# Moving the decay factors of a chunked linear attention to GpSimd, its result copies to ScalarE, and cutting its key-value product into 64x64 matmuls

## The chip, the cores and the metric

The kernel runs as one program on one core of one Trainium2 chip. The metric is the device time of one execution in microseconds (us). Three runs of the kernel before gave 903.01, 904.5 and 905.43 us; the median is 904.5 us.

The core has a matmul engine (TensorE, PE in the profile; its weight loads are shown as PEld), three engines for elementwise work (VectorE or DVE, ScalarE or ACT, GpSimd or POOL), and SyncE (SP), whose queue issues the DMAs here. Matmuls write PSUM banks; DVE and ACT read those banks; every operand of GpSimd in this kernel lies in SBUF.

## The reference

Three layers follow each other. The change touches the first one alone.

```python
# attention: q, k, v are (4 batches, 8 heads, 576 positions, 64)
scores = scale * np.matmul(q, k.transpose(0, 1, 3, 2))
gamma = 1.0 - 2.0 ** (-5.0 - np.arange(H, dtype=np.float32))
Dmat = np.where(rel >= 0, gamma[:, None, None] ** rel[None, :, :], 0.0)   # rel = i - j
attn = np.matmul(scores * Dmat[None], v)
# x = attn as 2304 tokens x 512
h = x @ w_in;  x = (h * np.cos(h)) @ w_out              # 512 -> 2048 -> 512
xn = x / rms(x) * rms_g
out = (silu(xn @ w_gate) * (xn @ w_val)) @ w_out2       # 512 -> 1536 -> 512
```

There is no softmax, so the decay gamma^(i-j) splits into gamma^i on the query side and gamma^(-j) on the values, and earlier positions can be summed up once as a state, the sum over j of key times value.

## The kernel before, in words

**Attention in 20 chunks.** Each batch is cut into five chunks of the sequence: four of 128 positions and a last one of 64 (`chunks`, `width`). `load(n)` brings a chunk in one DMA (the 64-wide one in two): keys `kt` and queries `qt` with the head dimension on the partitions, two heads per block of 128, values `vv` and keys once more `kk` with positions on the partitions. For each chunk:

- `scores(n)`: GpSimd multiplies the values by gamma^(-j) (L251); 8 matmuls make keys times queries, one per head, in 64-row halves of the array (L256), into two PSUM tiles; DVE copies each out through the causal mask (L259).
- `values(n)`: 4 matmuls of 128x128 add keys times values of each pair of heads to the tile `total` (L272), of which only the two 64x64 blocks on the diagonal are used; 4 matmuls apply the state of the earlier chunks to the queries (L277); ACT copies the two diagonal blocks of `total` into `state` (L282); 8 matmuls, one per head, add the masked scores times values (L287); DVE multiplies the result by `gam[c]`, which is gamma^i with the scale, on its way from PSUM to `xall` (L290). `gam[1]` to `gam[4]` are made once from `gam[0]` by ACT (L244).

All of this is in float32, so each of these matmuls shows twice in the trace: 8 matmuls are "x16".

**What runs beside it.** The first MLP goes in steps (token tile t, slice f of 128 hidden units). A step is 12 matmuls for the hidden slice (`hidden`, lines L193 to L195), the gate h*cos(h) on ACT and DVE (`gate_cos`: L431, L432, L434, L438, L440 and the difference on L130, which gives a high and a low part), and, three steps later, 12 matmuls of `out_t`. Weights arrive as 64-bit words of which float32 high and low parts are made (`Block.convert`: ACT L138, L147, L165; DVE L142, L143, L148, L149, L130), one block per hidden slice, 16 in all.

**Order of the work.** The first five chunks are the opening (`PRO`), with next to nothing beside them. Chunks 5 to 19 go two per step into steps 0 to 7 (`ATT_STEPS`), while the blocks are converted some steps ahead. After that the attention's PSUM and SBUF are given back, the last weight blocks are loaded, and the rest of the program (four more token tiles, the normalisation, the second MLP) follows. In this first part a scheduler puts each engine's instructions in one fixed order when the program is built; on the chip each engine works through its own list in that order and waits at an instruction until what it needs is there. Score tiles, attention results and hidden slices take turns in the three PSUM banks named `g` (`ps_tile`), so PE can begin a new one when an earlier one has been read out. SP's queue, in program order, loads chunk n+4 ahead of chunk n.

The lines that the change touches are L251 (behind it comes the new GpSimd instruction), L270 to L273 and L290.

Of the kernel before, what the change touches and what calls it, by code (L numbers as in the profile page):

```python
# [27 lines left out]
ALU = mybir.AluOpType  # L28
PSUM = bass.MemoryType.PSUM

P = 128
B, H, S, D = 4, 8, 576, 64
# [48 lines left out]
def body(ctx: ExitStack, tc, qkv, qkr, vr, w1, w2, rg, gq, gk, mask, out):  # L81
    nc = tc.nc
# [25 lines left out]
    def hidden_tile():  # L108
        return late["psh"].tile([P, 512], F32, tag="h", bufs=2, name="h")
# [4 lines left out]
    def ps_tile():  # L114
        if "psh" not in late:
            return psa.tile([P, 512], F32, tag="g", bufs=3, name="g")
        taken[0] += 1
        return hidden_tile() if taken[0] % 2 else acc_tile(KC + taken[0] // 2 % 2)
# [8 lines left out]
    xall = const.tile([P, KC, NT], F32, name="xall")  # L127
# [84 lines left out]
    ld, sc, total = {}, {}, {}  # L212
    gam0 = ap1.tile([P, NPAIR, P], F32, name="gam0")
    gam = [gam0]
# [31 lines left out]
    def scores(n):  # L246
        b, c = chunks[n]
        w = width(c)
        kt, qt, vv, _ = ld[n]
        v3 = vv[:w].rearrange("p (h d) -> p h d", h=H)  # L250
        nc.gpsimd.tensor_tensor(v3, v3, vg_sb[:w, c, :].unsqueeze(2).to_broadcast([w, H, D]), op=ALU.mult)  # L251
        ps = [ps_tile().rearrange("p (h i) -> p h i", h=NPAIR) for _ in range(2)]
        for p in range(NPAIR):
            for hh in range(2):
                r = slice(hh * D, (hh + 1) * D)
                nc.tensor.matmul(ps[hh][:w, p, :w], kt[r, p, :], qt[r, p, :], start=True, stop=True)  # L256
        for hh in range(2):
            s = ap.tile([P, NPAIR, P], F32, tag=f"s{hh}", bufs=2, name=f"s{hh}")
            nc.vector.tensor_tensor(s[:w, :, :w], ps[hh][:w, :, :w],  # L259
                                    mask_sb[:w, :w].unsqueeze(1).to_broadcast([w, NPAIR, w]), op=ALU.mult)  # L260
            sc[n, hh] = s

    def values(n):
        b, c = chunks[n]
        w = width(c)
        _, qt, vv, kk = ld.pop(n)
        if c < NFULL:
            if c == 0:
                total[0] = psa.tile([P, NPAIR, P], F32, tag="st", name="total")
            for p in range(NPAIR):  # L270
                cs = slice(p * P, (p + 1) * P)
                nc.tensor.matmul(total[0][:, p, :], kk[:, cs], vv[:, cs], start=c == 0 and p == 0, stop=True,  # L272
                                 skip_group_check=True)  # L273
        po = ps_tile().rearrange("p (a i) -> p a i", a=NPAIR)
        if c > 0:
            for p in range(NPAIR):
                nc.tensor.matmul(po[:, p, :w], state[:, p, :], qt[:, p, :], start=p == 0, stop=False,  # L277
                                 skip_group_check=True)
        if c < NFULL:
            for hh in range(2):  # L280
                r = slice(hh * D, (hh + 1) * D)
                nc.scalar.copy(state[r, :, r], total[0][r, :, r])  # L282
        for p in range(NPAIR):
            for hh in range(2):
                h = 2 * p + hh
                r = slice(hh * D, (hh + 1) * D)
                nc.tensor.matmul(po[r, p, :w], vv[:w, h * D:(h + 1) * D], sc[n, hh][:w, p, :w],  # L287
                                 start=c == 0 and p == 0, stop=True, skip_group_check=True)
        t0 = b * S + c * P
        nc.vector.tensor_tensor(xall[:, :, t0:t0 + w], po[:, :, :w], gam[c], op=ALU.mult)  # L290
        del sc[n, 0], sc[n, 1]

    warm = xsp.tile([P, 512], F32R, tag="xs", name="warm")
# [758 lines left out]
```

## Time and profile before

| | us |
|---|---|
| median of three runs | 904.5 (903.01 to 905.43) |
| the profiled execution, its own time | 904.74 |
| its span, first to last instruction | 902.9 |
| PE busy | 883.7 (98% of the span) |
| DVE busy | 669.0 (74%) |
| ACT busy | 478.3 (53%) |
| POOL busy | 96.3 (11%) |

The profiled execution is one run; 1.8 us of its time lie around the span. The attention takes the first 131 us of the span. Busy shares over the whole span say little about that stretch, so it is read by itself: the busy time of each engine between two points in time, then the instructions of one engine grouped by line and shape, then the order in time at single places. "A <- B" in a row of waits or in square brackets means that A stood idle until B had finished.

### The profile page before, as it was taken

What the parts mean: (1) busy time and instruction counts of PE and PEld (TensorE: products, weight loads), DVE (VectorE), ACT (ScalarE), POOL (GpSimd) and SP (SyncE); (2) the same over time, 40 slices, a digit from 0 to 9 for tenths busy, and PEclk for the clock granted to TensorE, in tenths of its full rate; (3) what the DMA queues carried; (4) which work ended last, traced back from release to release, by engine and by line L of the source; (5) the groups of instructions that cost most, each with busy time, mean ns of one, the idle gap of its engine ahead of it and who ended that gap; (6) DMA issues with size and microseconds to landing.
All of it is one profiled execution on the core that took longest, in us unless ns stands there. A gap on an engine that the chain in (4) does not pass through costs nothing.

```text
span 902.9 us, 14216 instructions
## 1 busy us (share of the span) xinstructions
PE 883.7 (98%) x5482; PEld 804.6 (89%) x5482; DVE 669.0 (74%) x999; ACT 478.3 (53%) x819; POOL 96.3 (11%) x99
## 2 busy tenths in 40 slices
PE   7999999999999999999999999999999999999998
PEld 6788778888887888998887899999999999999998
DVE  3999989678788887667777789789565589443584
ACT  4666566566565665456656665545443444333341
POOL 2331100000000000000434444200000000000000
PEclk9999999999999999999999999999999999999999
DMA  8966452044434444101568888998876788777793
GB/s 319 397 238 238 153 218 86 1 132 148 140 106 140 140 143 137 57 16 50 182 222 264 329 316 300 332 319 286 275 257 247 221 283 287 259 251 247 218 302 114
DMA packets 59027, 188.98 MB, mean 209 GB/s; under 512 B 5328, under 2 KB 23376, under 8 KB 50384
## 3 DMA queue, kind: packets, MB, share of 16 engines
q1 hardware_dynamic: 58960, 188.08, 61.2%
q8 instruction: 43, 0.70, 0.3%
q14 instruction: 24, 0.20, 0.1%
HBM read 140.87 MB, written 47.19 MB: 208 GB/s over the span
## 4 chain that ended last, share of the span: by engine, by line
PE 78%; DVE 14%; ACT 3%; issue 2%; DMA 1%; POOL 1%; SPq 0%; ACTq 0%; DVEq 0%; POOLq 0%
PE h L806 13%; PE acc L806 13%; PE acc L851 13%; PE acc L193 8%; PE acc L194 8%; PE acc L195 8%; PE h L193 3%; PE h L194 3%; PE h L195 3%; DVE w L130 3%; PE h L851 2%; DVE t L148 2%; DMA x<-qkv_dram 1%; DVE t L149 1%; PE g L287 1%
## 5 line engine op out<-in xcount | busy, mean ns | idle before, releaser
L806 PE MATMUL h<-w 128*128 128x384 f32 x720 | 139.9, 335 | 4.0 <-ACT s L772 2.7
L806 PE MATMUL acc<-w 128*128 128x384 f32 x720 | 140.1, 335 | 0.4
L806 PEld LDWEIGHTS h<-w 128*128 128x128 f32 x720 | 125.7, 188 | 5.9 <-ACT s L772 3.4
L806 PEld LDWEIGHTS acc<-w 128*128 128x128 f32 x720 | 125.5, 188 | 2.3 <-DVE v L794 2.3
L193 PE MATMUL acc<-ghi,w 128*128 128x512 f32 (+1 forms) x320 | 118.7, 371 | 1.5 <-ACT xall L662 1.4
L194 PE MATMUL acc<-glo,w 128*128 128x512 f32 (+1 forms) x320 | 118.2, 369 | 0.1
L195 PE MATMUL acc<-ghi,w 128*128 128x512 f32 (+1 forms) x320 | 117.8, 368 | 0.0
L851 PE MATMUL acc<-w 128*128 128x256 f32 x846 | 104.2, 283 | 0.0
L851 PEld LDWEIGHTS acc<-w 128*128 128x128 f32 x846 | 103.1, 191 | 0.3 <-DVE w L130 0.2
L434 ACT ACTIVATE r<-r,half_pi 128x512 f32<-128x512 f32 (+1 forms) x80 | 54.5, 681 | 61.7 <-DVE r L432 61.6
L529 POOL TENSOR_TENSOR z<-z 128x256 f32<-128x256 f32 x72 | 65.7, 914 | 156.7 <-DMA z<-w 94.4
L130 DVE TENSOR_TENSOR glo<-r,ghi 128x512 fp32r<-128x512 f32 (+1 forms) x78 | 52.2, 670 | 38.5 <-ACT ghi L440 38.0
L440 ACT CAST ghi<-r 128x512 fp32r<-128x512 f32 (+1 forms) x80 | 46.2, 577 | 54.8 <-DVE r L438 49.8
L193 PEld LDWEIGHTS acc<-ghi,w 128*128 128x128 f32 x320 | 60.3, 188 | 12.5 <-ACT xall L662 2.0
L195 PEld LDWEIGHTS acc<-ghi,w 128*128 128x128 f32 x320 | 60.3, 189 | 10.1
L194 PEld LDWEIGHTS acc<-glo,w 128*128 128x128 f32 x320 | 60.3, 188 | 10.0 <-DVE glo L130 0.3
L794 DVE TENSOR_TENSOR v<-s,acc 128x384 f32<-128x384 f32 x54 | 29.8, 552 | 52.7 <-PE acc L806 39.5
L834 ACT CAST w<-SV 128x768 fp32r<-128x768 f32 x55 | 42.4, 831 | 34.2 <-DVE SV L839 18.3
L130 DVE TENSOR_TENSOR w<-SV,w 128x768 fp32r<-128x768 f32 x55 | 50.1, 953 | 13.5 <-ACT w L834 13.5
L772 ACT COPY s<-h 128x384 f32<-128x384 f32 x54 | 25.8, 479 | 54.4 <-PE h L806 53.0
L193 PE MATMUL h<-xhi,w 128*128 128x512 f32 (+1 forms) x144 | 52.7, 366 | 0.0
L193 PE MATMUL acc<-xhi,w 128*128 128x512 f32 (+1 forms) x144 | 52.7, 366 | 0.0
(122 smaller groups left out, 1639.7 us busy)
## 6 DMA issues: line engine op xcount, KB each, us to landing
w<-so SPq DMA_DIRECT2D x42, 768.0 KB, 5.9
w<-s SPq DMA_DIRECT2D x24, 1024.0 KB, 4.9
raw<-w_dram SPq DMA_DIRECT2D x36, 512.0 KB, 4.1
w<-s SPq DMA_DIRECT2D x24, 768.0 KB, 4.3
raw<-w_dram SPq DMA_DIRECT2D x16, 1024.0 KB, 6.8
x<-qkv_dram SPq DMA_DIRECT2D x15, 1024.0 KB, 11.4
s<-w SPq DMA_DIRECT2D x12, 1024.0 KB, 6.2
w<-t SPq DMA_DIRECT2D x36, 256.0 KB, 2.4
```

The source lines that it names most:

```text
L130: eng.tensor_tensor(dst, src, hi.bitcast(F32), op=ALU.subtract)
L193: nc.tensor.matmul(dst, a[0], b[0], start=start, stop=False)
L194: nc.tensor.matmul(dst, a[0], b[1], start=False, stop=False)
L195: nc.tensor.matmul(dst, a[1], b[0], start=False, stop=stop)
L434: nc.scalar.activation(r, r, AF.Sin, bias=half_pi, scale=1.0)
L440: nc.scalar.copy(hi, r)
L529: nc.gpsimd.tensor_tensor(z[:, dst], z[:, a], z[:, b], op=op)
L772: nc.scalar.copy(t[:, :HALF], bank)
L794: nc.vector.tensor_tensor(t, s, bank, op=ALU.add)
L806: nc.tensor.matmul(bank, w[:, wp, kc * P:(kc + 1) * P], x[:, kc], start=k in (0, 1, 3) and kc == 0 and m == 0, stop=kc == 1 and m == 2, sk ...
L834: nc.scalar.copy(t[:, 0], src)
L851: nc.tensor.matmul(bank, s[:, a, i % 2, m * P:(m + 1) * P], wi[:, b], start=start and i == 0 and p == 0 and m % 2 == 0, stop=i == NPR - 1 ...
```

## The change

Four things change in `scores` and `values`:

1. Behind the scaling of the values, GpSimd multiplies the queries of the chunk in place by `gam[c]`, for all chunks but chunk 0. The score matmuls and the state matmuls then read scaled queries.
2. The result of every chunk but chunk 0 is copied from PSUM to `xall` by ACT, with no factor, in place of DVE's multiplication.
3. The product of keys and values is made per head: 8 matmuls of 64 columns by 64 columns in place of 4 of 128 by 128, the two heads of a pair in the two column halves of the array.
4. Chunk 0 keeps DVE's multiplication.

```diff
         nc.gpsimd.tensor_tensor(v3, v3, vg_sb[:w, c, :].unsqueeze(2).to_broadcast([w, H, D]), op=ALU.mult)
+        if n:
+            nc.gpsimd.tensor_tensor(qt, qt, gam[c], op=ALU.mult)
...
             for p in range(NPAIR):
-                cs = slice(p * P, (p + 1) * P)
-                nc.tensor.matmul(total[0][:, p, :], kk[:, cs], vv[:, cs], start=c == 0 and p == 0, stop=True,
-                                 skip_group_check=True)
+                for hh in range(2):
+                    h, r = 2 * p + hh, slice(hh * D, (hh + 1) * D)
+                    cs = slice(h * D, (h + 1) * D)
+                    nc.tensor.matmul(total[0][r, p, r], kk[:, cs], vv[:, cs], start=c == 0 and p == 0, stop=True,
+                                     skip_group_check=True)
...
-        nc.vector.tensor_tensor(xall[:, :, t0:t0 + w], po[:, :, :w], gam[c], op=ALU.mult)
+        if n:
+            nc.scalar.copy(xall[:, :, t0:t0 + w], po[:, :, :w])
+        else:
+            nc.vector.tensor_tensor(xall[:, :, t0:t0 + w], po[:, :, :w], gam[c], op=ALU.mult)
```

The scheduler lays the lists out anew. GpSimd's list for the first batch, as a difference (L251 scales values, the new L253 scales queries):

```order
-L251 TENSOR_TENSOR x<-x,gk_sb 128x512 x4
+L251 TENSOR_TENSOR x<-x,gk_sb 128x512 x2
+L253 TENSOR_TENSOR x<-x,gam_123 128x512
+L251 TENSOR_TENSOR x<-x,gk_sb 128x512
+L253 TENSOR_TENSOR x<-x,gam_145 128x512
+L251 TENSOR_TENSOR x<-x,gk_sb 128x512
+L253 TENSOR_TENSOR x<-x,gam_152 128x512
+L253 TENSOR_TENSOR x<-x,gam_162 128x256
 L251 TENSOR_TENSOR x<-x,gk_sb 64x512
```

Each scaling of queries stands directly behind (for the 64-wide chunk, ahead of) that of the chunk's values, and so ahead of the values of the next chunk.

DVE's list before, around the masks of chunk 6 (s_469 and s_471, L259) and the first gate (r, glo), with what each waits for:

```order
L290 TENSOR_TENSOR xall<-g,gam_162 128x4x64 [waits PE_49]
L142 TENSOR_SCALAR t<-t 128x1024
L259 TENSOR_TENSOR s_469<-g,mask_sb 128x512 [waits PE_49]
L143 TENSOR_SCALAR t<-t 128x1024 [waits DVE_49]
L148 SCALAR_TENSOR_TENSOR t<-raw,t 128x1024 [waits DMAHW6_49,DVE_49]
L432 SCALAR_TENSOR_TENSOR r<-r,g 128x512 [waits Activation_49]
L149 ISA t<-raw,t 128x2048 [waits DVE_49]
L259 TENSOR_TENSOR s_471<-g,mask_sb 128x512 [waits PE_49]
L438 TENSOR_TENSOR r<-g,r 128x512 [waits Activation_49]
L290 TENSOR_TENSOR xall<-g,gam_92 128x4x128 [waits PE_49]
L130 TENSOR_TENSOR w<-t,w 128x2x512 [waits Activation_49]
L130 TENSOR_TENSOR glo<-r,ghi 128x512 [waits Activation_49]
```

The same place in the changed kernel (the masks of chunk 6 are s_491 and s_493, L261; L439 and L445 are the old L432 and L438):

```order
L142 TENSOR_SCALAR t<-t 128x1024
L143 TENSOR_SCALAR t<-t 128x1024 [waits DVE_49]
L148 SCALAR_TENSOR_TENSOR t<-raw,t 128x1024 [waits DMAHW6_49,DVE_49]
L439 SCALAR_TENSOR_TENSOR r<-r,g 128x512 [waits Activation_49]
L149 ISA t<-raw,t 128x2048 [waits DVE_49]
L261 TENSOR_TENSOR s_491<-g,mask_sb 128x512 [waits PE_49]
L261 TENSOR_TENSOR s_493<-g,mask_sb 128x512 [waits PE_49]
L130 TENSOR_TENSOR w<-t,w 128x2x512 [waits Activation_49]
L445 TENSOR_TENSOR r<-g,r 128x512
L261 TENSOR_TENSOR s_531<-g,mask_sb 128x512 [waits PE_49]
L261 TENSOR_TENSOR s_533<-g,mask_sb 128x512 [waits PE_49]
L130 TENSOR_TENSOR glo<-r,ghi 128x512 [waits Activation_49]
```

The two results `xall` are gone from the list; the conversion of a block (L142, L143, L148, L149, then w) stands where it stood, and more of what is left lies between two steps of a conversion or a gate.

PE's list in the opening, changed kernel, from the products of chunk 0 on:

```order
L276 MATMUL total<-x 64x64 [waits DMAHW6_49,DMAHW4_49,Pool_49]
L276 MATMUL total<-x 64x64 x7
L258 MATMUL g<-x 128x128 [waits DMAHW7_49,Pool_49]
L258 MATMUL g<-x 128x128 [waits DVE_49]
L258 MATMUL g<-x 128x128 x6
L291 MATMUL g<-s_139,x 64x128 [waits DVE_49]
```

The scores of chunk 1 (L258, before L256) now wait for GpSimd as well as for their DMA, and chunk 0's own results (L291) stand behind them.

## Rows read from the trace of the kernel before

**Rows 1.** Busy us by stretch: PE, PEld, DVE, ACT, POOL; then clock, DMA, GB/s.

```profile
31.60:120.60 89.00, 84.58 (x734) 70.41 (x735) 87.64 (x115) 53.66 (x75) 19.52 (x13) 0.98 0.62 226
120.60:131.10 10.50, 10.50 (x79) 8.81 (x79) 7.89 (x12) 7.21 (x9) 0.00 (x0) 1.00 0.63 240
131.10:167.80 36.70, 36.70 (x163) 30.41 (x162) 33.19 (x43) 24.70 (x33) 0.00 (x0) 1.00 0.25 100
```

**Rows 2.** Timeline near the attention's end: start, us, engine, line, operation.

```profile
119.60 0.68 DVE L290 TENSOR_TENSOR xall<-g,gam 128x512 f32<-128x512 f32 x1
120.20 0.74 DVE L259 TENSOR_TENSOR s<-g,mask_sb 64x256 f32<-64x256 f32 x2
120.33 1.16 PE L277 MATMUL g<-x,state 128*128 128x128 f32 x8 [1.34 <-DVE xall L290]
122.45 0.50 PE L193 MATMUL g<-xhi,w 128*128 128x512 f32 x1
```

**Rows 3.** DVE from 24 to 131 us by line and shape: busy us, mean ns.

```profile
L149 DVE CUSTOM_DVE_ANT_0 t<-raw,t 128x2048 uint16<-128x2048 uint16 x12 | 15.4, 1283 | 0.0
L130 DVE TENSOR_TENSOR w<-t,w 128x1024 fp32r<-128x1024 f32 x10 | 14.6, 1462 | 0.0
L143 DVE TENSOR_SCALAR t<-t 128x1024 int32<-128x1024 int32 x11 | 8.4, 759 | 0.1
L130 DVE TENSOR_TENSOR glo<-r,ghi 128x512 fp32r<-128x512 f32 x7 | 5.6, 799 | 0.0
L130 DVE TENSOR_TENSOR xlo<-xall,xhi 128x512 fp32r<-128x512 f32 x4 | 3.8, 955 | 0.7 <-ACT xhi L187 0.7
```

**Rows 4.** Timeline, 31 to 35 us: DVE's differences beside one GpSimd scaling.

```profile
31.54 0.68 DVE L130 TENSOR_TENSOR xlo<-xall,xhi 128x512 fp32r<-128x512 f32 x1
32.14 1.21 DVE L130 TENSOR_TENSOR w<-t,w 128x1024 fp32r<-128x1024 f32 x1
32.27 1.98 POOL L251 TENSOR_TENSOR x<-x,gk_sb 128x512 f32<-128x512 f32 x1 [1.81 <-DMA x<-qkv_dram]
33.27 1.52 DVE L130 TENSOR_TENSOR xlo<-xall,xhi 128x512 fp32r<-128x512 f32 x1
```

**Rows 5.** Timeline, opening: chunk 1 and the factors.

```profile
9.53 4.57 ACT L244 ACTIVATE gam<-gam,gk_sb 128x128 f32<-128x128 f32 x16
...
11.38 1.69 PE L256 MATMUL g<-x 64*128 64x128 f32 x16 [1.28 <-DMA x<-qkv_dram]
11.40 1.04 POOL L251 TENSOR_TENSOR x<-x,gk_sb 128x512 f32<-128x512 f32 x1 [3.20 <-DMA x<-qkv_dram]
```

**Rows 6.** GpSimd from 24 to 131 us by line and shape.

```profile
L251 POOL TENSOR_TENSOR x<-x,gk_sb 128x512 f32<-128x512 f32 x12 | 17.2, 1432 | 52.1 <-DMA x<-qkv_dram 48.7 <-PE g L195 2.0 <-ACT state L282 1.4
L251 POOL TENSOR_TENSOR x<-x,gk_sb 64x512 f32<-64x512 f32 x3 | 4.9, 1617 | 11.8 <-DMA x<-vr_dram 11.8
```

**Rows 7.** GpSimd's products with two full operands, whole span: ns min/median/max, first and last start.

```profile
L130 POOL TENSOR_TENSOR glo<-r,ghi x2: 1304/1496/1688, 265.4 to 352.3; 128x512 fp32r<-128x512 f32 x2
L529 POOL TENSOR_TENSOR z<-z x72: 727/742/1528, 430.4 to 574.7; 128x256 f32<-128x256 f32 x72
```

**Rows 8.** ACT's copies of 128x512 from PSUM, later in the span.

```profile
L662 ACT COPY xall<-acc x20: 351/584/608, 191.2 to 507.6; 128x512 f32<-128x512 f32 x16, 128x256 f32<-128x256 f32 x4
```

**Rows 9.** A wait between 31.6 and 131 us: us in total, times, longest.

```profile
ACT state L282 <- PE g L277: 10.4, 7, 4.5
```

**Rows 10.** Timeline of PE in the opening, one group of matmuls per row.

```profile
20.44 1.16 PE L272 MATMUL total<-x 128*128 128x128 f32 x8
21.44 1.06 PE L277 MATMUL g<-x,state 128*128 128x128 f32 x8
22.43 1.09 PE L287 MATMUL g<-s,x 128*64 128x128 f32 x16
...
29.50 0.68 PE L287 MATMUL g<-s,x 64*64 64x64 f32 x16
```

**Rows 11.** PE in 3.5 us of the opening: busy, clock, DMA share, GB/s.

```profile
11.80:15.30 3.50, 3.50 (x32) 0.51 1.02 431
```

## The prediction

> **What bounds the kernel now.** Read the busy times by stretch first [rows 1]. From 131.10 us on PE is busy in all of the 36.70 us shown, and the rest of the span looks the same, so whatever moves the end of the attention moves the end of the program by as much. The question is what sets that end. Between 31.60 us (the second mask of chunk 5 is done) and 120.60 us (the first mask of chunk 19 is done) DVE is busy for 87.64 of 89.00 us, PE for 84.58, ACT for 53.66, GpSimd for 19.52. DVE is the one without room: it works through a fixed list and stands idle for 1.36 us of 89, so the time at which it reaches any mask is the sum of what stands ahead of it. PE idles for 4.42 us. The timeline shows what for [rows 2]: PE stands still for 1.34 us until DVE has read a result out at 119.60 + 0.68 us, then runs without a gap to the end (10.50 of 10.50 us, [rows 1]). The hidden slice of step 7 starts at 122.45 us and needs the bank that the first mask of chunk 19 gives back (120.20 us plus about half of 0.74, so 120.6): it had 1.8 us to spare. I therefore make the sum on DVE's list between those two masks, add what happens to the opening, and take off what PE can win behind the second mask.
>
> **Change part by part.**
>
> *DVE loses the results.* Between the two masks DVE's list held 113 rows; it holds 100 in the changed kernel. 11 results of 128x512 and 3 of 128x256 are gone, and one more step of a conversion (L149) stands ahead of chunk 19's mask. A result takes 0.68 us, but the next instruction starts 0.60 us after it (119.60 to 120.20, [rows 2]), so that a full one is worth 0.60 and a half one about 0.33: 11 x 0.60 + 3 x 0.33 = 7.6 us less. L149 takes 1.28 us [rows 3], some 1.1 at the pitch of a busy list: **-6.5 us**.
>
> *GpSimd gets 14 products in the same stretch* (chunks 6 to 19; five more come earlier). What do they cost DVE? Nothing if the engines did not meet; but they do [rows 4]. GpSimd's scaling takes 1.98 us there, where it takes 1.04 when nothing is in its way [rows 5]: it waited for DVE's `w` (two SBUF operands), and then DVE's `xlo` took 1.52 us where the one before took 0.68. So each waits for the other. Over 24 to 131 us DVE's two-operand instructions are longer than their undisturbed time (1.21 for `w`, 0.68 for `xlo` and `glo`, [rows 4]; I take `w`'s 1.21 for L149 and 0.68 for L143) by 10 x 0.25 + 4 x 0.27 + 7 x 0.12 + 12 x 0.07 + 11 x 0.08 = 6.1 us [rows 3]. 15 scalings of values ran there [rows 6], so one costs DVE 0.41 us, 39% of its own 1.04. The new products are longer: two full operands of 128x512 take GpSimd 1.30 us at least, and 128x256 take 0.73 [rows 7]; the values' factor is a broadcast and cheaper. 11 x 1.30 + 3 x 0.73 = 16.5 us of GpSimd, and 39% of it is 6.4. DVE's list also gets denser: of its rows in the stretch 58 of 113 had two SBUF operands (or were L142 and L143), now 59 of 100. Scaled by 0.59/0.51: **+7.4 us**. The bounds are 0 (each product meets only masks and gates, which read PSUM) and 16.5 (each stops DVE for its whole length); I stand at the rate the trace has for the same two engines in the same stretch. So DVE, relieved of 7.6 us, gets about as much back.
>
> The Trainium skill (SBUF — State Buffer, section Who interferes with whom) states this as a rule: a DVE instruction with two SBUF inputs, or in a 2-port mode, shares a port with GpSimd, and the second to issue fully blocks until the first is done. The trace agrees in kind (1.52 for 0.68 us). Taken to its end, every product stopping DVE for its whole length, it would put 16.5 in the place of 7.4 and make the sum +8.2 us; the mean that the trace shows, 0.41 of 1.04, makes it -0.9.
>
> *ACT gets 19 copies*, 0.58 us each [rows 8], 14 of them here: 7.8 us on an engine with 35 us free in the stretch [rows 1]. Its list is fixed too: the copy waits for L291, about 1 us behind the state's copies, and what stands behind it is late, while ACT already lost 10.4 us waiting for L277 to copy the state [rows 9]. What it feeds DVE are conversions, listed some steps ahead of their slice, and gates, so little should come through: **+0.5 us** (bounds 0 and 3).
>
> *PE's products per head.* 4 matmuls of 128 took 1.16 us of busy time; 8 matmuls of a head each, in two column halves, take 1.09 at 128 columns and 0.68 at 64 [rows 10]. The new ones have 64 columns and full rows; I take the 64-column row, about 0.45 less per chunk, some 5.4 us over the 12 chunks with this product from 5 to 18. If the halves did not overlap they would cost as much as now (bound 0). While DVE sets the pace this buys only the spare time at the end: PE arrives early at the bank of step 7's slice, at most **-1.8 us**. DVE's own 1.4 us of idle time, partly waits for PE, shrink: **-0.8**.
>
> The rule of the Trainium skill that speaks against this part is in TensorEngine Tiling (Array Packing), Tiling Modes, Key Properties: changing the tiling mode drains the engine, and the new form adds one change per chunk. The row shows such a change from L277 to L287: the former takes 0.99 us from start to start of the next for 8 records, as L272 takes 1.00 with no change of mode behind it [rows 10]; a drain of even 0.1 us would be 1.6 us in 16 chunks, and it would leave the sum as it is, since PE doesn't set it.
>
> *The opening.* Chunk 1's scores started at 11.38 us with their DMA [rows 5]; now they wait for the values' 1.04 and the queries' 1.30 us: 13.75, so 2.4 us late. `gam[1]`, the first four of 16 instructions from 9.53 on, is there by then. Ahead of chunk 2 to 5 PE gets 0.45 back each, and four results on ACT no longer hold up a bank, so that 0.3 us are left at chunk 5: **+0.3**. The bounds come from the clock: in 11.80 to 15.30 us it was granted at 0.51 (1.2 GHz), after PE had idled, and 32 matmuls went slowly [rows 11]. If PE's longer wait keeps it there for another such stretch, some 1.7 us are lost (+2); if not, and the pause swallows it, -0.5.
>
> *Behind the attention* nothing changes: the same conversions, 33.19 us of DVE beside 36.70 of PE [rows 1].
>
> **The sum:** +0.3 - 6.5 + 7.4 + 0.5 - 1.8 - 0.8 = -0.9 us. Against the profiled execution's 904.74 that is 903.8; that execution was 0.2 above the median, so against 904.5 I say **903.6 us**: no difference that could be measured (I count 0.3%, 2.7 us, as the least that a measurement of this kernel tells from none).
>
> **Rivals.**
>
> *A, DVE is only working ahead.* Its 98% are in part conversions made long before their use, and PE is busy for 95% of the stretch. If the scheduler's new list brings masks soon enough, PE sets the pace: 5.4 us of matmuls and about half of PE's 4.4 idle us [rows 1] go, less the opening: -7, **897.5 us**. For it: the waits for DVE are short, and the results that PE waited for last [rows 2] are no longer on DVE. Against: DVE's list cannot be left, and it has no idle time.
>
> *B, GpSimd blocks DVE harder.* Two scalings now follow each other, and a DVE instruction released by the first can be stopped by the second. At 80% of 16.5 us the cost is 13.2, not 7.4, and 5.8 more than the forecast are **909.4 us**. The balance turns at 50%: above that the products cost more than the results and the spare time at the end together give. For it: 0.84 us lost of 1.04 in [rows 4]. Against: the mean of all 15 is 0.41.
>
> *C, the opening.* The scores of each early chunk wait for GpSimd and PE's clock stays at 1.2 GHz for longer: +2 in place of +0.3, **905.5**.
>
> *D, the halves do not overlap*, so that PE gains nothing: no 1.8 at the end, **905.4**.
>
> **How the numbers follow.** Forecast 0.41, A 0.28, B 0.17, C 0.07, D 0.07. The forecast's own range is 900.5 to 907 and A and B stand at 897.5 and 909.4; with some room beyond each, since their prices are as rough as mine, 896.5 to 910 holds about 0.8. Faster by over 0.3% (under 901.8): A, nearly all, and 0.07 of the forecast, 0.34. Slower (over 907.2): B and 0.06 of the others, 0.23. The same: 0.43.
>
> **What would show it.** Right: GpSimd's new line at 1.3 us and more; DVE still busy for 97% between the two masks, with means of `w`, `xlo`, `glo` and L149 above those of [rows 3]; chunk 1's scores at about 13.8 us; the new product at about 0.68 us per chunk; no PE gap behind the attention, which ends within 2 us of 131.1. Wrong: DVE idle for several us between the masks (PE or ACT sets the pace), or an attention that ends before 127 or after 135 us.

## The result and the profile after

The changed kernel takes **916.0 us** (median of six runs, 913.56 to 917.61); the kernel before, on the same chip, 904.07 us (six runs, 903.01 to 906.5). The ratio is 1.0115, with a 95% interval of 1.0098 to 1.0133: slower by 11.9 us, outside the forecast's range, on the side of rival B.

The profiled execution of the changed kernel took 913.56 us (span 911.8), 8.8 us more than the profiled one of before; it is the quickest of the six, so about 3 us of the 11.9 lie in executions that left no trace (the two quickest had a mean granted clock of 0.990 and 0.991, the other four, 915.52 to 917.61 us, one of 0.986 or 0.987). Where the 8.8 us lie is told by cutting the span at the same events as in [rows 1]. Busy us of the changed kernel by stretch, columns as in [rows 1]; the cuts are the second mask of chunk 5, the first mask of chunk 19, and the first matmul of step 8:

```profile
33.36:127.61 94.25, 82.27 (x818) 65.53 (x818) 89.70 (x102) 58.45 (x86) 37.40 (x26) 0.95 0.56 201
127.61:138.00 10.39, 10.39 (x83) 8.73 (x80) 7.20 (x11) 8.60 (x12) 0.00 (x0) 1.00 0.64 254
138.00:175.10 37.10, 37.10 (x165) 30.75 (x164) 31.79 (x41) 24.14 (x32) 0.00 (x0) 1.00 0.26 100
```

The opening ends at 33.36 in place of 31.6 us: +1.8. The stretch between the two masks is 94.25 in place of 89.0 us: +5.3, of which DVE is busy for 2.1 us more (89.70 against 87.64) and idle for 3.2 us more (4.55 against 1.36). The tail to the attention's end is the same (10.39, 10.50). From there to the end it is 773.8 us (911.8 - 138.0) against 771.8: +2.0. Two signs of being wrong that the prediction names are there: DVE idle for several us between the masks, and an attention that ends after 135 us.

What DVE waits for between the two masks is PE's scores first and ACT second (us in total, times, longest):

```profile
DVE s L261 <- PE g L258: 2.5, 2, 1.9
DVE t L142 <- ACT t L138: 1.1, 2, 0.8
```

The stretch loses time in two ways. Its first part, up to the second mask of chunk 6, is this in the kernel before and in the changed one:

```profile
31.60:40.77 9.17, 7.51 (x52) 5.85 (x52) 9.13 (x13) 6.55 (x10) 3.78 (x2) 1.00 1.03 373
33.36:45.28 11.92, 6.85 (x52) 5.23 (x54) 11.43 (x12) 5.47 (x8) 8.96 (x8) 0.71 1.02 383
```

Here DVE is busy for 2.3 us more with one row less, beside a GpSimd that is busy for 8.96 us in place of 3.78. In the rest of the stretch DVE is busy for as long as before (78.27 against 78.50 us) and idle for 2.7 us more.

The two engines that meet in SBUF, 24 to 138 us. DVE by line and shape (busy us, mean ns, idle time before), to be held against [rows 3]:

```profile
L148 DVE SCALAR_TENSOR_TENSOR t<-raw,t 128x1024 int32<-128x1024 int32 x12 | 17.0, 1420 | 0.3
L149 DVE CUSTOM_DVE_ANT_0 t<-raw,t 128x2048 uint16<-128x2048 uint16 x12 | 16.9, 1405 | 0.2
L130 DVE TENSOR_TENSOR w<-t,w 128x1024 fp32r<-128x1024 f32 x11 | 16.1, 1473 | 0.0
L142 DVE TENSOR_SCALAR t<-t 128x1024 f32<-128x1024 f32 x13 | 13.2, 1017 | 4.0 <-ACT t L138 4.0
L143 DVE TENSOR_SCALAR t<-t 128x1024 int32<-128x1024 int32 x13 | 11.4, 880 | 0.2
```

L149 rises from 1283 to 1405 ns, L143 from 759 to 880, and, in the same view of the kernel before, L142 from 683 to 1017 and L148 from 1217 to 1420. `w` hardly rises (1462 to 1473) and `glo` falls (799 to 769). L142 also waits 4.0 us for ACT in this window, 1.1 us of it between the two masks. GpSimd in the same time (L253 is the new product, L251 the scaling of values, before 1432 and 1617 ns in [rows 6]):

```profile
L253 POOL TENSOR_TENSOR x<-x,gam 128x512 f32<-128x512 f32 x12 | 19.8, 1648 | 0.0
L253 POOL TENSOR_TENSOR x<-x,gam 128x256 f32<-128x256 f32 x3 | 3.7, 1241 | 5.4 <-DMA x<-qkr_dram 5.4
```

One meeting, at the first step of the MLP (timeline, columns as in [rows 2]; PE's L195 multiplies by the weights' low part `w`):

```profile
33.63 1.71 POOL L253 TENSOR_TENSOR x<-x,gam 128x512 f32<-128x512 f32 x1
34.14 2.28 DVE L130 TENSOR_TENSOR w<-t,w 128x1024 fp32r<-128x1024 f32 x1
...
36.47 0.80 PE L195 MATMUL g<-xhi,w 128*128 128x512 f32 x1 [3.14 <-DVE w L130]
```

`w`, 1.21 us in [rows 4], takes 2.28: it ends 1.08 us after the product does (35.34), so it stood still for nearly all of its overlap with the product. The rule of the Trainium skill (SBUF — State Buffer, Who interferes with whom), that the second to issue blocks fully, is what this pair shows. PE waits 3.14 us for `w`, about 1.1 of them owed to this standing still, and from 34.1 to 40.9 us PE's granted clock is 0.50 (1.2 GHz).

ACT's copies of the results, 24 to 138 us:

```profile
L295 ACT COPY xall<-g 128x512 f32<-128x512 f32 x14 | 8.2, 586 | 4.0 <-PE g L291 3.8
```

The opening (timeline) answers [rows 5]:

```profile
11.03 1.04 POOL L251 TENSOR_TENSOR x<-x,gk_sb 128x512 f32<-128x512 f32 x1 [3.25 <-DMA x<-qkv_dram]
12.03 1.26 POOL L253 TENSOR_TENSOR x<-x,gam 128x512 f32<-128x512 f32 x1
13.35 1.88 PE L258 MATMUL g<-x 64*128 64x128 f32 x16 [4.07 <-POOL x L253]
...
22.08 0.69 PE L276 MATMUL total<-x 128*64 128x64 f32 x16
```

Chunk 1's scores begin at 13.35 us in place of 11.38, behind the two GpSimd instructions; the new product per head takes 0.69 us a chunk in place of 1.16 [rows 10].

### The profile page after: what moved, and what is told of

Read it like the earlier page. It is cut to its first block, busy times and chain, and to the rows that moved or that the text cites. A ratio compares the mean times of both kernels' runs of the same rounds, so it can differ in the third digit from the quotient of the medians.

```text
span 911.8 us, 14476 instructions
## 1 busy us (share of the span) xinstructions
PE 883.2 (97%) x5610; PEld 800.8 (88%) x5610; DVE 669.3 (73%) x980; ACT 486.5 (53%) x838; POOL 123.7 (14%) x118
## 4 chain that ended last, share of the span: by engine, by line
PE 76%; DVE 13%; ACT 4%; issue 3%; DMA 2%; POOL 1%; SPq 1%; ACTq 0%; DVEq 0%; POOLq 0%
PE acc L858 13%; PE acc L813 12%; PE h L813 12%; PE acc L193 8%; PE acc L194 8%; PE acc L195 8%; PE h L193 3%; PE h L195 3%; PE h L194 3%; DVE w L130 2%; PE h L858 2%; DVE t L148 1%; DVE t L149 1%; DVE t L142 1%; DVE s L261 1%
## 5 line engine op out<-in xcount | busy, mean ns | idle before, releaser
L195 PE MATMUL acc<-ghi,w 128*128 128x512 f32 (+1 forms) x320 | 118.1, 369 | 0.0
L130 DVE TENSOR_TENSOR glo<-r,ghi 128x512 fp32r<-128x512 f32 (+1 forms) x78 | 52.0, 667 | 38.6 <-ACT ghi L447 38.0
L195 PEld LDWEIGHTS acc<-ghi,w 128*128 128x128 f32 x320 | 60.3, 189 | 10.2
L130 DVE TENSOR_TENSOR w<-SV,w 128x768 fp32r<-128x768 f32 x55 | 50.0, 953 | 13.5 <-ACT w L841 13.5
L194 PE MATMUL h<-xlo,w 128*128 128x512 f32 (+1 forms) x144 | 52.7, 366 | 0.0
```

The costliest lines, as they stand in the source:

```text
L130: eng.tensor_tensor(dst, src, hi.bitcast(F32), op=ALU.subtract)
L194: nc.tensor.matmul(dst, a[0], b[1], start=False, stop=False)
L195: nc.tensor.matmul(dst, a[1], b[0], start=False, stop=stop)
```

## The experiments

Two theories stood against each other. **The port theory:** the products themselves, by holding up DVE in SBUF, cost more than the relief gives. **The relief theory:** the port costs what was forecast or less; what failed is the relief (results to ACT, smaller products), which does not reach the time. "Copies" are the results that ACT copies out; a "conversion row" is one instruction of L142, L143, L148 or L149. All runs were compared with runs of the kernel before on the same chip: its medians were 904.9 us beside e1 to e4, 904.65 beside e5 to e8, 904.23 beside e9 to e12 and 905.48 beside e13 to e15. The table shows the time (median, n), its ratio, and from the profiled execution: the stretch from the second mask of chunk 5 to the first of chunk 19, DVE's busy and idle time in it, DVE's excess (sum over L142, L143, L148, L149 and the differences on L130 of the time above 0.68, 0.68, 1.22, 1.21, and 1.21 for `w` or 0.68 for `xlo` and `glo`), the mean granted clock there, and the attention's end.

```
                         us (n)      ratio [95%]               stretch  DVE busy/idle  excess  clock  end of att.
before                   904.07 (6)                             89.0    87.6 / 1.4      6.0    0.98   131.1
after                    916.0  (6)  1.0115 [1.0098, 1.0133]    94.3    89.7 / 4.5     13.7    0.95   138.0
e1_heads_only            911.12 (6)  1.0057 [1.0025, 1.0089]    96.8    86.7 / 10.0     6.0    0.91   137.9
e2_no_product            908.35 (10) 1.0037 [1.0024, 1.0049]    88.1    81.9 / 6.3      5.8    0.94   130.8
e3_product_aside         918.12 (4)  1.0142 [1.0102, 1.0182]    98.5    91.5 / 7.0     15.3    0.90   143.4
e4_write_only            906.78 (10) 1.0023 [1.0005, 1.0041]    88.8    84.2 / 4.6      7.6    0.98   130.2
e5_from_chunk5           917.4  (4)  1.0139 [1.0117, 1.0161]    99.1    94.2 / 4.8     14.6    0.91   142.6
e6_old_heads             919.54 (4)  1.0156 [1.0132, 1.0181]   100.4    93.1 / 7.3     12.7    0.93   144.4
e7_quadrants             909.32 (4)  1.0051 [1.0031, 1.0070]    93.1    88.9 / 4.2      5.4    0.98   135.9
e8_copies_only           911.8  (4)  1.0075 [1.0057, 1.0093]    96.2    87.0 / 9.2      6.7    0.95   136.6
e9_before_aside          916.84 (4)  1.0141 [1.0119, 1.0163]    95.2    93.4 / 1.8     11.7    0.95   138.3
e10_no_scaling           900.98 (11) 0.9962 [0.9949, 0.9975]    83.7    82.0 / 1.7      0.4    1.00   126.3
e11_copies_less_ahead    906.94 (12) 1.0026 [1.0016, 1.0035]    89.6    82.9 / 6.7      5.9    0.96   132.2
e12_before_less_ahead    906.08 (12) 1.0016 [1.0003, 1.0029]    88.7    85.5 / 3.2      5.6    0.98   131.1
e13_conversions_first    908.34 (10) 1.0030 [1.0015, 1.0046]    90.0    88.4 / 1.6      6.6    0.98   133.7
e14_out_last             905.25 (10) 1.0008 [0.9993, 1.0023]    85.1    83.9 / 1.1      4.6    1.00   129.0
e15_after_less_ahead     918.54 (4)  1.0147 [1.0124, 1.0171]    98.1    89.8 / 8.4     14.2    0.88   143.9
```

In e2, e3, e4, e8, e10 and e11 the factors in `gk` are all one, so the result has no decay. e3, e5, e6, e8, e9 and e15 came out above every range that had been expected for them.

### The product itself: left out, aside, or replaced by writes

e2 is the changed kernel without the product, e3 the same with the product written where nobody reads it, e4 the same with GpSimd kept busy by fills.

```diff
 # e2, against the changed kernel
-        if n:
-            nc.gpsimd.tensor_tensor(qt, qt, gam[c], op=ALU.mult)
-    gk = np.concatenate([vg.reshape(P, -1), later.reshape(P, -1)], 1).astype(np.float32)
+    gk = np.ones((P, NCH * (H + NPAIR)), np.float32)
 # e3, against e2
+        if n:
+            nc.gpsimd.tensor_tensor(aside[:, :, :w], qt, gam[c], op=ALU.mult)
```

e4 has `nc.gpsimd.memset` of `aside` in that place, three of 128x512 per chunk and two for a 64-wide one.

> The changed kernel without GpSimd's products on the queries; the decay factors are left out of the data (all ones), so that the result has no decay. Port theory (the products stop DVE's two-operand instructions, 10.7 us of it in the trace): the attention loses DVE's results and gets nothing back, 895 to 900 us. Wait theory (scores wait for GpSimd, PE idles, its clock falls): the same 895 to 900. List theory (the copies on ACT, in lists laid out anew, hold up what stands behind them): 908 to 914, the slowness stays.

> As the one without the products (decay left out of the data), but GpSimd makes each product at the same place in its list and writes it to a tile that nobody reads: the work without the wait. Port theory: nearly the changed kernel's time without what the opening lost, 909 to 914 us. Wait theory: as without the products, 895 to 900.

> As the one without the products (decay left out of the data), but GpSimd fills a tile that nobody reads, three times 128x512 (twice 128x256 for the short chunks), so it is about as busy but reads no SBUF. Port theory, if the port is that of reading: as without the products, 895 to 900 us. If GpSimd's writes, or its being busy, are enough: 905 to 914.

e2's and e3's instructions stand in the same order on DVE, ACT and PE, so the pair differs by the product alone, and nobody waits for its result: +9.8 us in the medians, +10.4 in the stretch, +9.5 in DVE's excess. DVE in the stretch up to the attention's end, e2:

```profile
L149 DVE CUSTOM_DVE_ANT_0 t<-raw,t 128x2048 uint16<-128x2048 uint16 x11 | 14.2, 1295 | 0.2
L130 DVE TENSOR_TENSOR w<-t,w 128x1024 fp32r<-128x1024 f32 x11 | 13.3, 1218 | 1.7 <-ACT w L165 1.7
```

and e3:

```profile
L149 DVE CUSTOM_DVE_ANT_0 t<-raw,t 128x2048 uint16<-128x2048 uint16 x11 | 16.9, 1534 | 0.2
L130 DVE TENSOR_TENSOR w<-t,w 128x1024 fp32r<-128x1024 f32 x11 | 15.7, 1431 | 1.8 <-ACT w L165 1.8
```

e4, with GpSimd busy for 31.07 of the stretch's 88.75 us against e2's 18.54 of 88.11, is no slower than e2 (906.78, 908.35). The ranges expected for e4 don't decide, since e2 itself did not come out at 895 to 900, and e4's lists are not those of e2. Its own trace says more: of the rows of DVE that count for the excess, 7 met only fills and are 0.4 us longer together, 22 met a scaling of values and are 7.0 us longer. A GpSimd that only writes costs DVE little; the product, which reads SBUF, costs 10 us in e3. But e2 also shows the second thing: with the product gone, DVE is busy for 5.8 us less than in the kernel before, and the time is still 3.45 us above it (908.35 against 904.9).

### The same two tests with the lists of the kernel before

e9 adds the product aside to the kernel before, e10 takes the scaling of values from it. In both, the instructions of DVE, ACT and PE stand in the same order as before.

```diff
 # e9
+        if n:
+            nc.gpsimd.tensor_tensor(aside[:, :, :w], qt, gam[c], op=ALU.mult)
 # e10
-        nc.gpsimd.tensor_tensor(v3, v3, vg_sb[:w, c, :].unsqueeze(2).to_broadcast([w, H, D]), op=ALU.mult)
-    gk = np.concatenate([vg.reshape(P, -1), later.reshape(P, -1)], 1).astype(np.float32)
+    gk = np.ones((P, NCH * (H + NPAIR)), np.float32)
```

> The kernel before, with GpSimd's product of queries and factors added and written to a tile that nobody reads; nothing else changes, and the instructions of DVE, ACT and PE stand in the same order as in the kernel before. Port theory (a two-operand product of GpSimd and DVE's two-operand instructions hold each other up): the third product aside beside an unchanged list of DVE, which has 1.4 us of idle time, should cost what it cost between the two kernels with and without it on the changed order (10.4 us of the stretch between the two masks, 9.8 of the time): attention's end at 138 to 142 us in place of 131.1, time 912 to 916 us, two-operand instructions of DVE 7 to 10 us longer in the stretch. Rival (the product costs by what waits for it, and nobody waits here; the 9.8 us came from the clock): within 2 us of the kernel before, 903 to 907 us.

> The kernel before without GpSimd's scaling of the values (all factors one: the decay is left out of the data), so that GpSimd does next to nothing beside DVE; the instructions of DVE, ACT and PE stand in the same order as before. Port theory: the 6.0 us by which DVE's two-operand instructions are longer than undisturbed in the stretch go; since PE idles for only 4.4 us of the stretch, 3 to 6 us of it reach the time: 899 to 902 us. Rival (PE and the waits between engines pace the attention already, so DVE's time is worth nothing below this): within 2 us of the kernel before, 903 to 906 us.

Busy us in the stretch, columns as in [rows 1], e9:

```profile
32.63:127.83 95.20, 87.73 (x732) 72.18 (x733) 93.41 (x115) 52.55 (x73) 39.65 (x26) 0.95 0.55 203
```

and e10, with GpSimd silent, and DVE's two-operand and conversion rows there up to the attention's end:

```profile
32.12:115.84 83.72, 82.68 (x734) 68.69 (x735) 82.01 (x114) 53.85 (x75) 0.00 (x0) 1.00 0.62 230
```

```profile
L148 DVE SCALAR_TENSOR_TENSOR t<-raw,t 128x1024 int32<-128x1024 int32 x11 | 13.4, 1220 | 0.1
L149 DVE CUSTOM_DVE_ANT_0 t<-raw,t 128x2048 uint16<-128x2048 uint16 x11 | 13.4, 1216 | 0.0
L130 DVE TENSOR_TENSOR w<-t,w 128x1024 fp32r<-128x1024 f32 x10 | 12.2, 1220 | 0.5 <-ACT w L165 0.4
L142 DVE TENSOR_SCALAR t<-t 128x1024 f32<-128x1024 f32 x12 | 8.2, 686 | 2.2 <-ACT t L138 2.2
L143 DVE TENSOR_SCALAR t<-t 128x1024 int32<-128x1024 int32 x11 | 7.5, 685 | 0.1
```

These are the undisturbed times. In the traces of the kernel before, the changed kernel, e2, e3 and e9, the rows of these lines and of L130 that no GpSimd instruction overlapped are together at most 0.25 us above them; the rest of the excess lies on rows that one overlapped. The masks, which read PSUM, take 0.69 us at most, overlapped or not. From e10 over the kernel before to e9, DVE's busy time in the same list goes 82.0, 87.6, 93.4 us, the stretch 83.7, 89.0, 95.2, and DVE's idle time stays at 1.4 to 1.8. As long as the list stands, a microsecond of port cost is a microsecond of the attention (e10's attention ends 4.8 us sooner; 3.25 us of that are left in the time). The product alone, read by nobody, makes the kernel before 12.6 us slower, as much as the whole change does. In the profiled execution it is 7.1 us (911.85 against 904.74); the other three of e9 took 915.85 to 918.07, and what is dearer in them isn't in a trace.

### The relief by itself: copies on ACT

e8 is the kernel before with the results copied by ACT and nothing else (no product, 128x128 products); e11 is e8 with one weight block less ahead of the attention's end.

```diff
 # e8 (and gk of ones, as in e2)
-        nc.vector.tensor_tensor(xall[:, :, t0:t0 + w], po[:, :, :w], gam[c], op=ALU.mult)
+        if n:
+            nc.scalar.copy(xall[:, :, t0:t0 + w], po[:, :, :w])
+        else:
+            nc.vector.tensor_tensor(xall[:, :, t0:t0 + w], po[:, :, :w], gam[c], op=ALU.mult)
 # e11, against e8; e12 and e15 have the same PLAN
-PLAN = [0, 1, 2, 3, -1, 4, 5, -1, 6, 7, -1, 8, -1, 9, 10, -1, -1, 11, 12, -1, 13, 14, -1, -1, 15, 16, -1, 17, 18, -1, 19]
+PLAN = [0, 1, 2, 3, -1, 4, 5, -1, 6, 7, -1, 8, -1, 9, 10, -1, 11, 12, -1, 13, 14, -1, -1, 15, 16, -1, 17, 18, -1, 19]
```

> The kernel before with ACT copying the results out and no products on GpSimd (the decay is left out of the data), products of keys and values 128x128 as before. If DVE's list sets the pace and the product per head was what kept the kernel without the GpSimd products at 908: 897 to 902 us. List theory (ACT's copies and the lists laid out anew cost what DVE gains): 905 to 910.

> The kernel with the result copies on ACT alone (decay left out of the data, no product on GpSimd, 128x128 products of keys and values), with one weight block less loaded ahead of the attention's end. Its DVE order has 40 rows of conversions (L142, L143, L148, L149) between the two masks, the same kernel with all blocks had 44, the kernel before 39. List theory (ACT's copies cost nothing; the 7 us came from conversions that the new order puts ahead of the last masks): four rows of about 1.0 us less, attention's end at 131 to 133 us in place of 136.6, time 905 to 908 us. Rival (ACT works in order, the copies wait for PE there and what DVE needs from ACT comes late): 910 to 913 us, DVE idle for 8 us and more between the masks as before.

With no product and no port cost beyond that of before, e8 is 7 us slower than the kernel before. Its stretch, then e11's (columns as in [rows 1]):

```profile
31.33:127.51 96.18, 86.03 (x748) 71.57 (x750) 86.99 (x105) 61.00 (x92) 17.38 (x13) 0.95 0.59 220
```

```profile
31.34:120.95 89.61, 82.85 (x729) 68.60 (x730) 82.88 (x101) 58.72 (x88) 19.23 (x13) 0.96 0.59 218
```

The scheduler filled the room that the results left on DVE: 44 conversion rows (L142, L143, L148, L149) stand between the masks in e8, 39 in the kernel before. With 40 of them, in e11, 4.9 us of the medians come back (4.4 by the two ratios), as the list theory said. What remains is the point: in e11 DVE is busy for 4.8 us less than before and idle for 5.4 us more, and the kernel is still 2.7 us slower. What DVE waits for (e8, 31.33 to 127.51 us; us in total, times, longest) is ACT, 8.4 us of 8.6 in the rows of this view:

```profile
DVE t L142 <- ACT t L138: 4.8, 5, 1.9
DVE r L435 <- ACT r L434: 1.5, 2, 1.0
DVE glo L130 <- ACT ghi L443: 1.2, 2, 0.6
```

How ACT comes to be late, and how DVE runs dry, is seen in e11's timeline. Two places:

```profile
41.57 0.72 ACT L437 ACTIVATE r<-r,half_pi 128x512 f32<-128x512 f32 x1
42.20 1.11 ACT L138 ACTIVATE t<-raw 128x1024 f32<-128x1024 f32 x1
43.22 0.57 ACT L291 COPY xall<-g 128x512 f32<-128x512 f32 x1
43.84 0.59 PE L256 MATMUL g<-x 64*128 64x128 f32 x2 [2.30 <-ACT xall L291]
...
112.96 0.69 ACT L434 ACTIVATE r<-g,quarter 128x512 int32<-128x512 f32 x1 [2.37 <-PE g L195]
113.68 0.69 DVE L435 SCALAR_TENSOR_TENSOR r<-r,g 128x512 f32<-128x512 int32 x1 [3.14 <-ACT r L434]
```

At 41.5 us the chunk's result is ready (PE waits from there on), but the copy stands behind a sine and a conversion step in ACT's list, and PE loses 2.30 us for a bank. At 110.5 us DVE is through with what it has and waits 3.14 us for the gate, which waits for PE's hidden slice. DVE, made quicker, arrives earlier at an instruction whose input is made by others.

### New lists with the same work

To tell the copies from the mere fact of a new list, e13 and e14 keep all work and only change where the program issues it; e12 has the shorter PLAN in the kernel before, e15 in the changed kernel.

```diff
 # e13: conversions moved ahead of out_t and values; e14: out_t moved behind them
+        if first:
+            while converted[0] < min(len(blocks1), i + CONV_LEAD + 1):
+                blocks1[converted[0]].convert(temps())
+                converted[0] += 1
         if i >= LAG:
             out_t(*steps[i - LAG])
         if more:
             values(more[0])
```

> The kernel before with one weight block less loaded ahead of the attention's end, nothing else; its DVE order has 36 rows of conversions between the two masks in place of 39. List theory: the attention ends 2 to 4 us sooner (127 to 129 us), and the time is that much lower if the conversion finds room behind the attention, where DVE was busy for 33.2 of 36.7 us: 901 to 904 us. Rival (PE paces the attention, or the block comes too late for its slice): 904 to 908 us.

> The kernel before with the same work, written in another order: in each step the conversion of a weight block is issued ahead of the first MLP's second product and the attention's values, not behind them, so that the scheduler lays the lists of DVE, ACT and PE out anew (113 rows of DVE between the two masks, as before). Theory that a new list alone brings waits: DVE idle for 3 to 6 us in place of 1.4 between the masks, time 906 to 910 us. Rival (the idle time came with the copies on ACT, which wait there for PE in front of what DVE needs): DVE idle for at most 2.5 us, time 903 to 906 us.

> The kernel before with the same work, written in another order: in each step the first MLP's second product is issued behind the attention's values and the conversions. The lists are laid out anew, with 3 rows less of DVE between the two masks (110 in place of 113). New-list theory: DVE idle for 3 to 6 us, time 905 to 910 us in spite of the 3 rows. Rival (only the copies on ACT make it wait): idle at most 2.5 us and the attention's end 1 to 3 us sooner, 901 to 904.5 us.

> The changed kernel with one weight block less loaded ahead of the attention's end (39 conversion rows L142 to L149 between the two masks in place of 40; in the kernel with the copies alone this edit took 4 rows and 4.9 us). List theory by rows: 1 row less, 914 to 916 us, and all that is left above the kernel before is the product's cost, 8 to 12 us. Rival (the edit helps by spreading the loads, not by rows): 910 to 912 us.

e13 and e14 have new lists, and DVE idles for 1.6 and 1.1 us, as the rivals expected, while the times, 908.34 and 905.25 us, lie in the ranges of the new-list theory. So a new list need not bring waits. But it can: e1 and e7, the next section's runs, take nothing off DVE and have new lists too, since they issue two and four times the matmuls of one product, and DVE idles for 10.0 and 4.2 us. That the waits of e2, e8 and e11 come from the copies alone is therefore not shown. e13's time rises by 2.9 us in steps of about a microsecond in opening, stretch and tail and behind them. e14's attention ends 2.1 us sooner and the time stays (905.25, 905.48). Of the 2.6 us that its trace loses behind the attention, 1.9 lie in the second MLP, where PE runs at 1.2 GHz from 501.1 to 504.5 us (granted clock 0.50); only what is left can be rows that DVE does behind the mask. In e12 DVE is busy for 2.1 us less and idle for 1.8 us more, the attention ends where it did, and the time is 1.9 us higher, in the rival's range. e15 missed both expectations: 918.54 us, with the clock at 0.88 in the stretch and DVE idle for 8.4 us. The edit that repaired e8 doesn't repair the changed kernel.

### The smaller products

e1 puts the product per head into the kernel before; e7 makes all four 64x64 blocks of each pair there; e6 puts the 128x128 product back into the changed kernel.

```diff
 # e1 (e7 also makes the two blocks off the diagonal; e6 undoes this in the changed kernel)
-                cs = slice(p * P, (p + 1) * P)
-                nc.tensor.matmul(total[0][:, p, :], kk[:, cs], vv[:, cs], start=c == 0 and p == 0, stop=True,
-                                 skip_group_check=True)
+                for hh in range(2):
+                    h, r = 2 * p + hh, slice(hh * D, (hh + 1) * D)
+                    cs = slice(h * D, (h + 1) * D)
+                    nc.tensor.matmul(total[0][r, p, r], kk[:, cs], vv[:, cs], start=c == 0 and p == 0, stop=True,
+                                     skip_group_check=True)
```

> The kernel before with the product of keys and values per head alone; GpSimd and DVE do what they did. If DVE's list sets the attention's pace and GpSimd's products were what made the change slow (port theory), 901.5 to 904.5 us against 904.1: PE has 5.4 us less to do and gets at most the 1.8 at the end. If the new matmul form itself costs time (a drain per change of tiling mode, or lists that the scheduler lays out worse with 64 more instructions), 906 to 912.

> The kernel before with all four 64x64 blocks of each pair's product made by matmuls of 64x64, 16 per chunk: the new form, but as much work for PE as before. Clock theory (PE's missing work): 903 to 907 us, mean clock near 0.995 as before. If the form itself (column halves, changes of the tiling mode, twice the instructions) is what cost the kernel with the product per head alone its 6 us: 909 to 914.

> The changed kernel with the product of keys and values as 4 matmuls of 128x128 again. Clock theory (shorter products let PE idle longer between waits, and the granted clock falls more often): 909 to 913 us, with a mean clock above 0.990. Port theory alone, by which PE's work does not matter: 915 to 918.

In the kernel before, the product per head costs 6.2 us in the medians and 5.2 by the ratio (e1: 911.12, but its runs reach from 904.29 at a mean clock of 0.992 to 912.74 at 0.986). Beside ACT's copies the kernels with it are quicker (e8 911.8 to e2 908.35; e6 919.54 to after 916.0), but there the lists differ in more than the product: e8 and e6 have 44 conversion rows between the masks, e2 and the changed kernel 40. e11, with the 128x128 product and 40 rows, is no slower than e2 (906.94, 908.35), so a gain from the smaller product itself is not shown. A lower clock is not the whole reason for the cost: e7, which makes the whole product as the kernel before does and has a clock of 0.998 over the span, is 4.7 us slower too. In e1 the clock of the stretch is 0.91, and what that costs is not told apart from what the new list costs. Why this part costs in the kernel before stays open.

### The opening

e5 is the changed kernel with products and copies from chunk 5 on alone (`if n >= PRO`).

> The changed kernel with the products on GpSimd and the copies on ACT from chunk 5 on only; the opening multiplies on DVE as before. The opening lost 1.75 us and one stretch at 1.2 GHz in the changed kernel's trace. Port theory: 912 to 915 us against 916, most of the loss stays, since it comes from the products of chunks 5 to 19. If the wait of the early scores for GpSimd and the fall of the clock behind it were the main cause: 904 to 909.

The opening ends 0.7 us earlier (32.6 against 33.4 us) and the stretch is 4.8 us longer; the time, 917.4, is not better. e5's lists are new as well, with 43 conversion rows between the masks in place of 40, so it doesn't price the opening cleanly; but most of the loss does not come from there.

## Why the prediction was wrong

**The step that failed is the credit.** The forecast had -6.5 (results off DVE), -1.8 (PE's spare time at the end) and -0.8 (DVE's idle time) on one side, +7.4 for the port on the other. e2 is the change without its product. By the terms of the forecast, the copies' +0.5 included, it should have been 8.6 us faster than the kernel before; it is 3.45 us slower. That is 12.0 of the 12.8 us between the forecast -0.9 and the measured +11.9. The product, with the opening's wait for it, takes e2's +3.45 to +11.9: 8.5 us, forecast 7.7 (the lists of the two differ). Against the kernel before the product is the larger part of the loss; against the forecast the credit is. The credit was taken as time because "the time at which it reaches any mask is the sum of what stands ahead of it". That holds for instructions that get shorter in an unchanged list (e10: 5.6 us less busy, stretch 5.3 us shorter). It does not hold for work handed to ACT: e11 and e2 take 4.8 and 5.8 us of busy time off DVE with no product in the way, and the stretch is 0.6 longer and 0.9 us shorter. It does not hold in e12 either (2.1 us less busy, stretch 0.3 us shorter), and it does in e14 (3.7 less, 3.9 shorter). DVE's idle time of 1.4 us was read as the mark of an engine without room; it was also that of a list whose inputs are ready in time. Relieved, DVE waits: for ACT in e8 (8.4 us), for PE's scores (2.5) and ACT (1.5) in the changed kernel. That the credit did not come is shown; how much of it is owed to the copies' place in ACT's list, how much to the new lists and how much to the lower clock is not.

Term by term, in the profiled executions:

- *DVE's rows, -6.5 + 7.4 = +0.9:* measured +2.1 of busy time. The excess rose by 7.7 us (6.0 to 13.7), forecast 7.4; e9 gives 5.7 and e3 against e2 9.5. The price of the port, taken from the mean of 15 scalings, was about right for DVE's rows, in part by luck: it was taken from `w`, `xlo`, `glo`, L149 and L143, of which `w` hardly rose and `glo` fell, and most of the rise is on L142 and L148, which had no share in it. As time the product costs more: 9.8 and 12.6 us in the medians of the two pairs that differ by it alone. Rival B, 909.4, was the nearest, and in e9 the product does cost about the 13.2 us that it named; but B kept the credit, and that is most of the difference.
- *DVE's idle time, -0.8:* +3.2, 4 us off. *PE's spare time, -1.8:* nothing; the tail is 10.39 against 10.50 us, and PE, which in the forecast arrived early, waits for masks and `w` in the stretch (idle for 12.0 us, before 4.4).
- *ACT's copies, +0.5, bounds 0 and 3:* the copies run at 0.586 us as forecast, but e8 puts the move as a whole (relief included) at +7 us, e11 at +2.7. The runs measure copies and relief together: either ACT's lateness cost far more than the bound of 3, or the relief was worth nothing. They don't tell the two apart.
- *The opening, +0.3:* +1.8, inside the bounds given. Chunk 1's scores came at 13.35 us (forecast 13.75); 0.69 us per product matched 0.68. The time forecast to be won back by chunk 5 was not. Rival C's mechanism is not there: in the traced executions the clock of the opening is 0.91 from chunk 1's scores on, before 0.92 (and by C's own terms its 905.5 is 905.3).
- *The clock of the stretch, not in the sum:* it fell from 0.98 to 0.95. PE ran at 1.2 GHz for 10.2 us of the stretch, before for 3.4; in e2, e8 and e9 for 10.2, in e1 for 17.1, in e3 for 20.5, in e10 and e14 not at all. No run changes the clock alone, so what it costs, and what of it only follows PE's waits, stays open.
- *Behind the attention, nothing:* +2.0. A piece at 1.2 GHz (clock 0.50) lies where the second MLP begins; the profiled execution of before has none there:

```profile
505.10:508.50 3.40, 3.34 (x11) 2.82 (x10) 0.97 (x3) 1.26 (x3) 2.45 (x3) 0.50 0.98 381
```

  In the 10 us ahead of it PE was busy for 7.83 us; nine of the 17 traces have such a piece there, e10, e12 and e14 among them, so it isn't a mark of the change. About 1.4 of the 2.0 us lie in the second MLP. That the end of the program moves by as much as the end of the attention, as the prediction has it, holds to about 3 us: what lies behind the attention is between 0.7 us shorter (e5) and 2.8 us longer (e10) than in the kernel before.

These add up: 1.8 + 2.1 + 3.2 - 0.1 + 2.0 = 9.0, measured 8.8 (the cuts are rounded).

Rival A (DVE only works ahead, PE paces) was right that DVE's load alone does not set the time, but wrong about what does: not PE's pace with 7 us won, but waits between ACT, DVE and PE, with a lower mean clock beside them. Rival D falls: the halves overlap (0.69 us).

## What to carry to other kernels

An engine that is busy for 98% in a fixed list was here a bound upwards and not downwards: what lengthened its instructions was paid in full, while work handed to another engine brought no time. Before counting such a credit, look at whether the other engines' lists deliver what the relieved engine needs as much earlier. Price the two directions apart, and test the relief by itself (the copies without the product) before setting it against a cost. An elementwise product on GpSimd that reads SBUF is not free beside DVE even if nobody waits for it: here 15 products of 1.26 us and 4 of 0.73, 22 us of GpSimd, cost 9.8 and 12.6 us in the two pairs of runs that differ by them alone.

## What was not expected of the hardware

GpSimd's fills, which only write SBUF, cost DVE little (e4: excess 7.6 us against e2's 5.8 with GpSimd busy for 12.5 us more, and 0.4 us on the rows that met fills alone), while its two-operand products cost 9.5 in e3 (19.7 us more). DVE's one-operand conversion steps are held up as well: L142 takes 686 ns with GpSimd silent (e10) and 1017 in the changed kernel, L143 685 and 880.

The scaling of values that was always there costs the kernel before 3.3 us (e10, ratio 0.9962); no other place for it was tried. No kernel here that does the whole computation was faster than the kernel before.
